# A third pair of score-row buffers, a 136-column memory update and a new order table in an Infini-attention and FNet kernel

## The chip, the cores and the metric

The kernel runs on one NeuronCore of one Trainium2 chip. The metric is the device time of one launch in microseconds (us); the time before is the median of three runs. Engines are named as in the profile: PE (matrix multiply, with PEld for the loads of its stationary operand), DVE (vector), ACT (scalar), POOL (GpSimd) and SP, whose queue issues all the DMAs here.

## What is computed

The input `x` is 2048 rows of 512. Two layers follow each other, each of them a memory attention `A` and a Fourier mixing `B`, both on a layer-normed input and both with a residual:

```python
x = x + _A_ref(_layernorm(x), wq, wk, wv, wo, beta)
x = x + _B_ref(_layernorm(x), dft_seq_re, dft_seq_im, dft_hid_re, dft_hid_im)
...
# A: 32 heads of width 16, 4 segments of 512 rows
for s in range(N):
    qs, ks, vs = q[:, :, s], k[:, :, s], v[:, :, s]
    logits = einsum("bhqd,bhkd->bhqk", qs, ks) * scale + mask     # causal
    a_dot = einsum("bhqk,bhkd->bhqd", softmax(logits), vs)
    pq = phi(qs)                                                   # t+1 or exp(t)
    a_mem = einsum("bhld,bhde->bhle", pq, M) / (einsum("bhld,bhd->bhl", pq, z)[..., None] + 1e-6)
    outs.append(g * a_mem + (1.0 - g) * a_dot)
    pk = phi(ks)
    M = M + einsum("bhld,bhle->bhde", pk, vs)
    z = z + einsum("bhld->bhd", pk)
# B: y = Cr @ (x @ Hr^T) - Ci @ (x @ Hi^T)
```

## The kernel before

**Units of work.** A layer has four segments of 512 rows and four groups of 8 heads, so there are 32 units `i` (segment `q = i // 4`, group `g = i % 4`). All products that need accuracy are made of fp16 pairs: a value is split into a high half and a low half, and three matmuls (`mm3`, line 370) replace one. For a unit the kernel makes q and k (`s_p`, line 784), writes their split halves to DRAM and reads them back in another arrangement, two heads of a pair in partitions 0 to 47 and 64 to 111 (`t_split`, line 681). The tiles that receive them are the row buffers `qst` and `kst`, two of each (`NR = 2`), taken in turn as `i % NR`.

**Scores, maxima, probabilities.** `s_x` (line 895) makes the scores with queries on partitions, and DVE takes the maximum of each row (`t_max`, line 884, 32 instructions for a unit; each writes a `junk` tile of which there are two). The maxima are transposed on PE, split, and sent by DMA into two more rows of `qst`. `s_st` (line 946) then makes the scores once more, transposed and with the maximum subtracted; ACT takes the exponential and POOL the causal mask (`t_sel`). `s_av` (line 969) multiplies the probabilities with the values: the stationary operand is `vt`, 32 columns in fp32 (16 values of a head and 16 ones, whose product is the softmax denominator), and four heads go to four column groups of the array. A buffer pair comes free when `s_st` of its unit is done: in `t_split`, line 703, unit `i` waits on `("ST", i - 2)` before its read-back is issued.

**Memory.** `s_mem` (line 838) reads the memory of a group (`macc`) and updates it: for segments 0 to 2 of each layer, 24 units in all, four matmuls with `phi(k)` as stationary operand stream `vt`, which is laid out per pair of heads as values, ones, values (3 x 16 columns, times 4 pairs: 192 columns in fp32). DVE multiplies the result by the block mask `bd`. In the trace every fp32 matmul stands as two instructions.

**Start.** The layer norms of a segment are in `t_ln` (line 585): statistics on DVE, three small instructions on POOL, then ACT, and a subtraction on POOL or DVE, whichever the planner finds free (`tt`, line 360). For the first segment of each layer (`direct`) the result is transposed on PE. Beside this the weights are loaded into parts of the tile `y`, scaled and split (`s_w`, `s_wo`, `share`). `vt` and `y` are plain SBUF tiles; `y` is free of other use in rows 8 to 11 from the time that the value weights are split until segment 2 writes its rows.

**What sets the order.** Instructions of an engine run in the order in which the program issues them. That order is found at build time: the streams (`s_...`) and tasks (`t_...`) are generators that yield at each step what engine and data they need, and a planner (`Plan`, line 50) with a cost for each instruction picks the step that can start first. The table `LEAN` (line 33) adds a bias in ns for a stream and engine (`t_splitV=-40` puts DVE's step of `t_split` 40 ns behind). Where PE would be idle for long the planner puts in matmuls without use (`t_warm`, line 1216, tile `onesb`). Changing any cost or bias can change the order of the whole program.

Of the kernel before, what the change touches and what calls it, by code (L numbers as in the profile page):

```python
# [19 lines left out]
TT = L // 128  # L20
# [12 lines left out]
LEAN = dict(s_stT=150.0, s_memV=40.0, s_wV=80.0, s_rY=150.0, t_mergeA=40.0, s_xA=150.0, t_abA=40.0, t_mergeY=-150.0, s_mV=40.0, t_cV=-40.0, s_cA=-80.0, s_oY=40.0, t_cY=80.0, t_lnG=80.0, t_splitV=-40.0, t_phiA=150.0, s_kV=-300.0, t_mergeV=150.0, s_cT=80.0, s_avT=80.0, s_wA=-150.0, t_resV=-150.0, t_selG=40.0, s_lnY=-150.0, t_rowsY=300.0, t_ktY=-80.0)  # L33
# [9 lines left out]
PHM, EARLYLN, FEW = 5, 1, 0  # L43
WARM, IDLE, SPARE = 4200, 500.0, 300.0
# [5 lines left out]
class Plan:  # L50
# [31 lines left out]
    def key(self, a):  # L82
        f = self.fine.get(a.tensor.name)
        return (a.tensor.name, a.offset // f) if f else a.tensor.name
# [70 lines left out]
    def op(self, eng, name, args, kw):  # L155
# [19 lines left out]
        elif eng == "A":  # L175
            c = n / 1.2 + (52 if src else 93) + (93 if any(a.free_size() == 1 for a in ins) else 0)
        elif eng == "V":
# [9 lines left out]
        elif eng == "G":  # L187
            c = 127 + n * 0.915 if name == "affine_select" else 96 + n * 2.1
            if name == "tensor_tensor" and kw.get("op") == OP.pow:
                c = 300 + n * 165  # L190
            elif name == "partition_all_reduce":
                c = 370
# [86 lines left out]
def body(ctx: ExitStack, tc: tile.TileContext, x, wq, wk, wv, wo, beta, wd, cs, out):  # L279
# [61 lines left out]
    vt = [const.tile([128, TT, NP, 3, 16], F32, name=f"vt{i}") for i in range(NR)]  # L341
# [5 lines left out]
    bd = const.tile([128, 2, 4, 32], F32, name="bd")  # L347
# [65 lines left out]
    def share(o, src, s):  # L413
        yield need("A", src, s)
        A.activation(o[:, 0], src, AF.Copy, scale=s)
        A.activation(src, src, AF.Copy, scale=s)
        yield need("VG", o, src)
        tt(o[:, 1], src, o[:, 0], OP.subtract)

# [105 lines left out]
    def t_ones():  # L525
# [8 lines left out]
        for i in range(NR):  # L534
            for a in range(2):
                yield need("Y", d8, mode="b")
                Y.dma_start(kst[i][64 * a + 48:64 * a + 50].rearrange("r p n -> r (p n)"), d8, est=(415, 341, 472))
        done.add("KR")

    def s_k():  # L540
# [12 lines left out]
        for j in range(NR):  # L553
            V.memset(vt[j][:, :, :, 1, :], 1.0)
        done.add("VI")
        yield need("V")
        bits(rp, 3, 1.0)
        bits(ra, 64, 1.0 / 64)
        cj = sb("en", F32, (128, 2, 4, 32))
# [25 lines left out]
    def t_ln(src, xi, dst, key, direct=False):  # L585
        st = rg("bst", 2, F32, (128, 6))
        V.bn_stats(st, src)
        mv = rg("mv", 6, F32, (128, 4))
        V.bn_aggr(mv[:, 0:2], st)
        yield need("G", mv)  # L590
        rs = rg("rs", 6, F32, (128, 1))
        G.tensor_scalar(mv[:, 2:3], mv[:, 1:2], 1e-5, 2.0 ** -20, op0=OP.add, op1=OP.mult)
        G.tensor_tensor(rs, mv[:, 2:3], mhalf, op=OP.pow)
        G.tensor_scalar(mv[:, 3:4], mv[:, 0:1], rs, -1.0, op0=OP.mult, op1=OP.mult)
# [6 lines left out]
        else:  # L601
            A.activation(hl[:, 0], xi, AF.Copy)
        yield need("VG", xi, hl)
        tt(hl[:, 1], xi, hl[:, 0], OP.subtract)
        pl.close(xi)
        if direct:
# [7 lines left out]
            if pl.free["A"] <= pl.free["V"]:  # L614
# [36 lines left out]
    def t_merge(e, o, gi, g, n, key):  # L651
# [7 lines left out]
        rc = rg("rc", 4, F32, (128, 2, 16))  # L659
        xa = x[:, 0]  # L660

        def view(off, *dims):
            return bass.AP(xa.tensor, xa.offset + off, [list(xa.ap[0])] + [list(d) for d in dims])

        yield need("V", x)
        d = view(16, (496, 2), (32, 16))
        if not gi:
            V.tensor_scalar(rc, d, 1e-6, None, op0=OP.add)
            d = rc
# [4 lines left out]
        for a in range(2):  # L674
            c = slice(16 * a, 16 * a + 16)
            tt(n.rearrange("p (b r) -> p b r", r=32)[:, :, c], view(528 * a, (32, 16), (1, 16)),
# [4 lines left out]
    def t_split(p, key, f, kphi):  # L681
# [24 lines left out]
        dst = (qst if order else kst)[i % NR]  # L706
# [621 lines left out]
```

## Time and profile before

| | |
|---|---|
| time, median of 3 runs | 1695.57 us (1693.65 to 1700.11) |
| the profiled execution's own time | 1699.92 us |
| its span, first to last instruction | 1698.2 us |
| mean granted TensorE clock in it | 0.989 |
| PE busy | 1662.3 us (98%) |
| DVE, ACT, POOL busy | 1036.8, 872.3, 810.3 us |

The page of the profile gives busy times, the span in 40 slices, the chain of work that ended last and the costliest groups. A row of a group holds, behind the bar, busy time and mean ns of one instruction, and behind the second bar the idle time before. A row of the timeline holds the start, the length of the run, the engine, the instruction with its output and inputs, and its count; brackets give idle time before it and what ended it. A row of the table by stretches gives busy time and count for each engine, the granted clock, the DMA share and GB/s. Nearly all instructions go through one helper and so have one line (L272); they are told apart by tile. In the profile's names a matmul `b<-kst,qst` with 48 rows is one of `s_x`, and `b<-qst,kst` with 50 rows is one of `s_st`; `b<-w,vt` is `s_av`, `b<-vt,w` the memory update.

### The profile page before, as it was taken

The numbers are of one execution on the slowest core, as the hardware profiler recorded it, in microseconds if no ns is written. First come the engines' busy times: TensorE is split into PE (matmuls) and PEld (weight loads), VectorE is DVE, ScalarE is ACT, GpSimd is POOL, SyncE is SP. The second block draws the span as 40 slices with busy tenths as digits, with TensorE's granted clock in tenths as the row PEclk, the third lists the DMA queues.
The fourth block names the chain that finished last, engine by engine and source line by source line (L and its number), as shares of the span: only waits on it lengthen the run. The fifth ranks groups of instructions, "written<-read, shape, count | busy, mean of one in ns | idle before, by whom it ended". The sixth has DMA issues, their size and how long they took to land.

```text
span 1698.2 us, 32247 instructions
## 1 busy us (share of the span) xinstructions
PE 1662.3 (98%) x11145; PEld 734.7 (43%) x11145; DVE 1036.8 (61%) x3262; ACT 872.3 (51%) x1480; POOL 810.3 (48%) x1445
## 2 busy tenths in 40 slices
PE   8889999999999999999999999999999999999999
PEld 4344344444444344444544444443444444444444
DVE  8784865778677786635768558546575765433221
ACT  5487577755656666535376754655455325312000
POOL 4376556575565556634255644635454415322000
PEclk9789999999999999999999999999999999999999
DMA  7546545655357432525746663543435322131423
GB/s 182 147 116 178 128 132 159 172 142 152 94 148 208 126 119 84 189 56 196 193 148 187 182 179 90 132 116 98 140 91 149 105 85 76 57 125 38 143 70 123
DMA packets 208629, 222.92 MB, mean 131 GB/s; under 512 B 104520, under 2 KB 127048, under 8 KB 208464
## 3 DMA queue, kind: packets, MB, share of 16 engines
q1 hardware_dynamic: 208464, 220.85, 45.8%
q8 instruction: 88, 1.44, 0.4%
q14 instruction: 77, 0.63, 0.1%
HBM read 137.40 MB, written 61.87 MB: 117 GB/s over the span
## 4 chain that ended last, share of the span: by engine, by line
PE 77%; DVE 9%; ACT 5%; issue 4%; DMA 3%; POOL 2%; SPq 1%; ACTq 0%; DVEq 0%; POOLq 0%
PE b L272 77%; ACT w L272 4%; DVE junk L272 4%; SPq L272 1%; DVE w L272 1%; POOL w L272 1%; DMA w<-w 1%; DMA w<-x 1%; DVE m L272 1%; DVE mx L272 1%; DVE y L272 1%; DVE bst L272 0%; DVE cam L272 0%; DMA w<-in_cs_dram 0%; DVE pmax L272 0%
## 5 line engine op out<-in xcount | busy, mean ns | idle before, releaser
L272 PEld LDWEIGHTS <-w 128*128 128x128 f16 x5056 | 467.8, 98 | 612.8 <-issue 101.1
L272 PE MATMUL b<-w,w 128*128 128x512 f16 x3072 | 708.5, 380 | 1.7 <-DVE mx L272 0.8
L272 ACT ACTIVATE w<-b,fac 128x512 f32<-128x512 f32 (+1 forms) x728 | 419.2, 655 | 176.3 <-PE b L272 175.8
L272 DVE CUSTOM_DVE_ANT_0 junk<-b,cmask 128x128 bf16<-128x128 f32 (+3 forms) x1024 | 436.3, 483 | 71.6 <-PE b L272 71.1
L272 POOL TENSOR_TENSOR w<-w,w 128x512 f16<-128x512 f32 (+1 forms) x294 | 347.5, 1187 | 247.1 <-ACT w L272 223.6
L272 POOL TENSOR_SCALAR_AFFINE_SELECT w<-w 128x128 f32<-128x128 f32 (+2 forms) x704 | 237.0, 350 | 202.7 <-ACT w L272 194.1
L272 DVE SCALAR_TENSOR_TENSOR y<-b,fyu,y 128x512 f32<-128x512 f32 x200 | 148.9, 745 | 235.6 <-PE b L272 235.2
L272 ACT ACTIVATE w<-w,csc 128x512 f16<-128x512 f32 (+1 forms) x256 | 180.1, 720 | 41.5 <-DVE csc L272 32.8
L272 PE MATMUL b<-g,w 128*128 128x512 f16 x768 | 183.1, 383 | 3.2 <-DMA g<-w 0.8
L272 PE MATMUL b<-wd,w 128*128 128x512 f16 x768 | 176.8, 379 | 0.1
L272 PE MATMUL b<-w,vt 128*32 128x512 f32 (+3 forms) x2048 | 172.4, 449 | 1.9 <-POOL w L272 1.1
L272 ACT ACTIVATE w<-b 128x512 f16<-128x512 f32 x128 | 75.9, 596 | 189.4 <-PE b L272 179.3
L272 DVE SCALAR_TENSOR_TENSOR w<-b,w 128x512 f16<-128x512 f32 x128 | 87.6, 687 | 120.3 <-ACT w L272 118.7
L272 ACT ACTIVATE w<-w 128x512 f16<-128x512 f32 (+1 forms) x137 | 86.5, 632 | 90.1 <-DVE w L272 87.9
L272 PE MATMUL b<-kst,qst 48*128 48x128 f16 (+3 forms) x1024 | 117.5, 304 | 6.3 <-DVE mx L272 3.2
L272 PE MATMUL b<-qst,kst 50*128 50x512 f16 (+3 forms) x1024 | 115.8, 302 | 5.5 <-DVE mx L272 2.2
L272 PE MATMUL b<-w,g 128*128 128x128 f16 x1536 | 96.3, 221 | 0.0
L272 PEld LDWEIGHTS <-g 128*128 128x128 f16 x1536 | 89.6, 99 | 12.7 <-issue 7.8
L272 DVE STREAM_TRANSPOSE m<-b 128x512 f32<-128x512 f32 x112 | 75.6, 698 | 31.1 <-PE b L272 30.7
L272 PEld LDWEIGHTS b<-w,vt 128*32 128x32 f32 x2048 | 54.8, 110 | 87.7 <-issue 48.2
L272 PE MATMUL b<-wo,w 128*128 128x512 f16 x384 | 89.1, 379 | 0.0
L272 PEld LDWEIGHTS <-kst 50*128 50x128 f16 x1024 | 37.3, 94 | 111.7 <-issue 105.2
(105 smaller groups left out, 1019.3 us busy)
## 6 DMA issues: line engine op xcount, KB each, us to landing
w<-in_cs_dram SPq DMA_DIRECT2D x128, 256.0 KB, 3.5
cc<-w SPq DMA_DIRECT2D x128, 256.0 KB, 3.2
w<-cc SPq DMA_DIRECT2D x128, 256.0 KB, 3.1
w<-w SPq DMA_DIRECT2D x96, 256.0 KB, 3.5
d<-w SPq DMA_DIRECT2D x128, 128.0 KB, 2.5
w<-in_x_dram SPq DMA_DIRECT2D x32, 256.0 KB, 3.6
qst<-d SPq DMA_DIRECT2D x64, 128.0 KB, 2.7
kst<-d SPq DMA_DIRECT2D x64, 128.0 KB, 3.3
```

The costliest lines, as they stand in the source:

```text
L272: r = f(*args, **kw)
```

## The change

The title given with the change is: third pair of row buffers for group 2, update by 136 columns, first norms on DVE, steps of one tile apart, new table; two junk tiles for the maxima. The line of the junk tiles is the same in both kernels (two).

- **Row buffers.** A third `kst` and `qst` lie in rows 8 to 11 of `y`, for unit 2 alone (`ring`). Unit 2 waits for the value weights (`("W", 2, g)`) in place of `("ST", 0)`; unit 3 waits on `("ST", 0)` and unit 4 on `("ST", 1)`; from unit 5 on it is two units back as before.
- **Update.** `vt` becomes [tile, 32, 8]: 16 value columns and 16 columns of ones, each by 8 heads, with the heads innermost. The update streams 17 x 8 = 136 columns. `s_av` takes the 32 columns of a head at a step of 8 elements (32 bytes). The value weights are permuted on the host to suit, and ACT writes `vt` in one stretch. DVE's mask step reads the result at a step of 8, once for the values and once, broadcast, for the ones; `bd` becomes bf16.
- **First norms.** For `direct` norms two of the three small instructions go to DVE, and so does the subtraction.
- **Steps apart.** Extra `yield`s (`YL`, `YB`, `YM`, `YC`, `YS`) let the planner put other work between dependent instructions of one tile.
- **Planner.** A new `LEAN`, more cost for an ACT instruction with a bias tile, more latency for small POOL instructions, a preference for DVE in copying the first transposes, and unused matmuls before the causal mask is there.
- **Buffers.** `mx`, `mhl` and `rc` have half as many.

```diff
-LEAN = dict(... t_abA=40.0, ... s_oY=40.0, ... s_cT=80.0, ...)
+LEAN = dict(... t_abA=150.0, ... s_cT=150.0, ... s_ldY=300.0, t_lnA=80.0, t_lnY=-150.0)
...
+            if name == "activation" and isinstance(kw.get("bias"), bass.AP):
+                c += 80
...
+            if n <= 32:
+                lat = 172
...
-    vt = [const.tile([128, TT, NP, 3, 16], F32, name=f"vt{i}") for i in range(NR)]
+    kst.append(y[:, 8:10, :].bitcast(F16).rearrange("p a (b n) -> p (a b) n", n=512))
+    qst.append(y[:, 10:12, :].bitcast(F16).rearrange("p a (b n) -> p (a b) n", n=512))
+    ring = [0, 1, 2] + [(i - 3) % 2 for i in range(3, NGRP)]
+    prior = [None] * 3 + [0, 1] + list(range(3, NGRP - 2))
+    vt = [const.tile([128, TT, 32, HG], F32, name=f"vt{i}") for i in range(NR)]
...
-    bd = const.tile([128, 2, 4, 32], F32, name="bd")
+    bd = const.tile([128, 2, 4, 32], BF16, name="bd")
...
         A.activation(o[:, 0], src, AF.Copy, scale=s)
+        if YC:
+            yield need("A", o)
         A.activation(src, src, AF.Copy, scale=s)
...
+        if direct and STARTV:
+            yield need("V", mv)
+            V.tensor_scalar(mv[:, 2:3], mv[:, 1:2], 1e-5, 2.0 ** -20, op0=OP.add, op1=OP.mult)
+            yield need("G", mv)
+            G.tensor_tensor(rs, mv[:, 2:3], mhalf, op=OP.pow)
+            yield need("V", mv, rs)
+            V.tensor_scalar(mv[:, 3:4], mv[:, 0:1], rs, -1.0, op0=OP.mult, op1=OP.mult)
...
-        yield need("VG", xi, hl)
-        tt(hl[:, 1], xi, hl[:, 0], OP.subtract)
+        if direct:
+            yield need("V", xi, hl)
+            V.tensor_tensor(hl[:, 1], xi, hl[:, 0], op=OP.subtract)
+        else:
+            yield need("VG", xi, hl)
+            tt(hl[:, 1], xi, hl[:, 0], OP.subtract)
...
-        if i >= NR:
-            yield gate(("ST", i - NR))
+        if i == NR:
+            yield gate(*[("W", 2, g) for g in range(NG)])
+        elif i > NR:
+            yield gate(("ST", prior[i]))
...
-        A.activation(vt[i % NR].rearrange("p t j e d -> p (t j) e d")[:, :, 0:3:2, :],
-                     p.rearrange("p t (j e d) -> p (t j) e d", j=NP, e=2), AF.Copy, scale=2.0 ** -24)
+        A.activation(vt[i % NR].rearrange("p t d h -> p t (d h)")[:, :, :128], p, AF.Copy, scale=2.0 ** -24)
...
-                mp = ps("pj", F32, (128, NP, 48))
+                mp = ps("pj", F32, (128, 17, HG))
...
-                    T.matmul(mp, phk[:, 128 * t:128 * t + 128], v[:, t], start=(t == 0), stop=(t == TT - 1))
+                    T.matmul(mp, phk[:, 128 * t:128 * t + 128], v[:, t, :17], start=(t == 0), stop=(t == TT - 1))
...
-                for a in range(2):
-                    V.tensor_tensor(mu[:, a], mp[:, :, 16 * a:16 * a + 32], bd[:, a], op=OP.mult)
+                for e, d in ((0, HG), (16, 0)):
+                    V.tensor_tensor(view(mu, e, (128, 2), (32, NP), (1, 16)),
+                                    view(mp, HG * e, (NP, 2), (1, NP), (d, 16)),
+                                    view(bd, e, (128, 2), (32, NP), (1, 16)), op=OP.mult)
...
-            mx = rg("mx", 2, F32, (128, 2, NP, TT))
+            mx = rg("mx", 1, F32, (128, 2, NP, TT))
...
-                                 v[:, t, p].rearrange("k e d -> k (e d)")[:, 16 * a:16 * a + 32], tiles[p][1],
+                                 v[:, t, :, NP * a + p], tiles[p][1],
...
-        if "CM" not in done or at - pl.free["T"] < IDLE or pl.lately(at) >= WARM:
+        if at - pl.free["T"] < IDLE or pl.lately(at) >= WARM:
```

More of the change, by code (lines that the diff above doesn't have):

```diff
@@ L418, in share, with view @@
         tt(o[:, 1], src, o[:, 0], OP.subtract)
+    def view(t, off, *dims):
+        return bass.AP(t.tensor, t.offset + off, [list(t.ap[0])] + [list(d) for d in dims])
     def flat(t):
@@ L658, in t_merge @@
         pl.close(e, o)
[L659 to L663, printed above, removed]
+        rc = rg("rc", 2, F32, (128, 2, 16))
         yield need("V", x)
[L666 removed]
+        d = view(x, 16, (512, 2), (32, 16))
         if not gi:
             V.tensor_scalar(rc, d, 1e-6, None, op0=OP.add)
+            if YM:
+                yield need("V", rc)
             d = rc
@@ L701, in t_split @@
             spawn(t_kt(hl, kphi))
-        if i >= NR:
-            yield gate(("ST", i - NR))
+        if i == NR:
+            yield gate(*[("W", 2, g) for g in range(NG)])
+        elif i > NR:
+            yield gate(("ST", prior[i]))
         yield need("Y", d)
         order = key[0] == "dq"
-        dst = (qst if order else kst)[i % NR]
+        dst = (qst if order else kst)[ring[i]]
         for a in range(2):
```

55 lines of the change are left out of this document (38 added, 17 removed).

## Prediction

> **What bounds the kernel now.** First the page: which engine is never free, and where its clock falls. Then the table by stretches, which says whether PE's idle time is spread or in one place.
>
> ```profile
> span 1698.2 us, 32247 instructions
> PE 1662.3 (98%) x11145; PEld 734.7 (43%) x11145; DVE 1036.8 (61%) x3262; ACT 872.3 (51%) x1480; POOL 810.3 (48%) x1445
> PEclk9789999999999999999999999999999999999999
> ```
>
> ```profile
> 0.00:20.00 20.00, 14.34 (x77) 6.53 (x78) 16.96 (x53) 9.84 (x12) 10.07 (x25) 1.00 0.82 211
> 20.00:45.00 25.00, 24.22 (x197) 12.96 (x195) 23.38 (x93) 13.92 (x24) 8.10 (x7) 1.00 0.67 157
> 45.00:140.00 95.00, 83.78 (x587) 33.78 (x586) 69.08 (x270) 68.47 (x120) 58.90 (x112) 0.82 0.46 125
> 200.00:1600.00 1400.00, 1387.91 (x9435) 612.28 (x9434) 864.91 (x2673) 742.78 (x1262) 696.33 (x1241) 1.00 0.45 129
> 900.00:1000.00 100.00, 97.84 (x725) 44.43 (x726) 65.21 (x224) 63.18 (x108) 56.42 (x102) 1.00 0.64 180
> ```
>
> From 200 to 1600 us PE idles 12.1 of 1400 us at full clock: what PE does there is paid for one to one, and what the other engines do there is free until one of them becomes late. The start is different. From 45 to 140 us PE idles 11.2 of 95 us and the granted clock is 0.82, so another 0.18 x 95 = 17 us of cycles are gone, and its 587 instructions are 6.2 a us against 9435 / 1400 = 6.7 later. This part is held by something else. So the change has two places to act: PE's own work anywhere, and the chain of the start.
>
> **The update.** These rows hold what the narrower update is worth: 24 units x 4 matmuls x 2 instructions.
>
> ```profile
> L272 PE MATMUL b<-vt,w 128*128 128x192 f32 x192 | 38.6, 338 | 1.4 <-ACT vt L272 1.2 <-POOL w L272 0.2
> L272 PEld LDWEIGHTS b<-w,vt 128*32 128x32 f32 x2048 | 54.8, 110 | 87.7 <-issue 48.2 <-POOL w L272 23.4 <-DVE mx L272 3.0
> L272 PEld LDWEIGHTS b<-vt,w 128*128 128x128 f32 x192 | 30.9, 190 | 10.7 <-issue 2.7 <-DVE mx L272 2.3 <-ACT vt L272 1.6
> ```
>
> ```profile
> 75.16 1.07 PE L272 MATMUL b<-w,vt 128*32 128x512 f32 x8
> 79.55 1.57 PE L272 MATMUL b<-vt,w 128*128 128x192 f32 x8
> 81.05 0.85 PE L272 MATMUL b<-w,vt 128*32 128x384 f32 x8
> 82.16 0.92 PE L272 MATMUL b<-vt,w 128*128 128x192 f32 x4
> ```
>
> The mean of 338 ns holds the way through the array, which overlaps. The pace is in the runs: (1.57 - 0.92) / 4 = 162.5 ns each, 0.85 ns a column. 136 columns then take 115 ns, 47 ns less, and 192 x 47 ns = 9.1 us, all in PE's time. One thing could stop it short: the load of the next stationary operand. A 128-column fp32 load takes 190 ns and a 32-column one 110, so 80 / 96 = 0.83 ns a column and 107 ns for 128 columns: still under 115. I take -9.1 us. ACT's write of `vt` and DVE's mask step keep their element counts and are off PE's path; ends 0 and, if each of the 48 mask instructions were late on an idle PE, a few us in the start, so 0.
>
> **Weights at a step of 32 bytes.** `s_av` pays for the same layout: each head's 32 fp32 weights now lie 8 elements apart. The trace has only packed loads: 54.8 us / 2048 = 27 ns each where they run one behind the other. A burst of `s_av` is four heads in two rounds. The second round's loads lie under the first round's stream: 512 columns and 384 columns differ by 0.22 us over two rounds, so 128 columns take 0.11 us a round. Only the first loads of a burst are open, and there are 32 units x 4 tiles x 2 halves = 256 bursts. A load of n times the length costs 256 x 27 x (n - 1) ns: 0 for n = 1, 6.9 us for n = 2, 28 us for n = 5. A gain is excluded, since packed loads are the best case here. I take 0, the row that the trace has, and keep 6.9 us for the range.
>
> [...]
>
> **The third buffer pair.** What did unit 2 wait for? PE first: the end of unit 1's maxima (the transpose of `mx`), the last scores of `s_st` of unit 0, and the units 2 and 3 of `s_x`. Then SP and DVE.
>
> ```profile
> 69.74 0.39 PE L272 MATMUL b<-identf,mx 128*32 128x128 f32 x1 [1.56 <-DVE mx L272]
> 83.01 0.40 PE L272 MATMUL b<-qst,kst 50*128 50x128 f16 x8
> 90.67 0.42 PE L272 MATMUL b<-kst,qst 48*128 48x128 f16 x8
> 112.56 0.27 PE L272 MATMUL b<-identf,mx 128*32 128x128 f32 x1
> 113.44 0.61 PE L272 MATMUL b<-kst,qst 48*128 48x128 f16 x12
> 131.24 0.27 PE L272 MATMUL b<-identf,mx 128*32 128x128 f32 x1 [0.94 <-ACT w L272]
> 138.71 2.10 PE L272 MATMUL b<-g,w 128*128 128x512 f16 x9
> ```
>
> ```profile
> 72.97 2.63 SPq L272 DMA_DIRECT2D d<-w  x4
> 75.70 1.36 SPq L272 DMA_TRANSPOSE w<-w  x1
> 77.11 0.57 SPq L272 DMA_DIRECT2D w<-in_x_dram  x1
> 79.76 3.05 SPq L272 DMA_DIRECT2D d<-w  x4
> 83.43 1.74 SPq L272 DMA_DIRECT2D qst<-d  x4
> 85.21 1.81 SPq L272 DMA_DIRECT2D kst<-d  x4
> ...
> 104.04 1.71 SPq L272 DMA_DIRECT2D qst<-d  x4
> 110.14 0.46 SPq L272 DMA_DIRECT2D w<-in_x_dram  x1
> ```
>
> ```profile
> 70.67 0.67 DVE L272 SCALAR_TENSOR_TENSOR w<-b,w 128x512 f16<-128x512 f32 x1
> 71.98 0.69 DVE L272 SCALAR_TENSOR_TENSOR w<-b,w 128x512 f16<-128x512 f32 x1
> 79.04 0.69 DVE L272 SCALAR_TENSOR_TENSOR w<-b,w 128x512 f16<-128x512 f32 x1 [6.37 <-ACT w L272]
> ```
>
> ```profile
> 59.01 1.16 POOL L272 TENSOR_TENSOR w<-y,w 128x512 f16<-128x512 f32 x1 [0.21 <-ACT y L272]
> ```
>
> ```profile
> d<-w SPq DMA_DIRECT2D x128, 128.0 KB, 2.5
> kst<-d SPq DMA_DIRECT2D x64, 128.0 KB, 3.3
> ```
>
> The read-back of unit 2 is issued at 83.43, at the end of `s_st` of unit 0 (83.01 + 0.40). So the wait is real. But behind it stands another: DVE makes the low halves of unit 2 only at 70.67 and 71.98, after all maxima of unit 1, and the write to DRAM leaves SP at 72.97 to 75.60 and lands 2.5 us later, at 78.1. `t_splitV` stays at -40 in the new table, so I leave that order. With the gate gone the read-back can be issued at 78.1, behind the transpose and the x load that SP holds until 77.7; it takes 1.74 + 1.81 us, and the last part lands 3.3 us after its issue, at about 85. Unit 2's scores start there and not at 90.67: 5.4 us sooner. They then take what they took, 112.56 - 90.67 = 21.9 us, and so end at 107; unit 3's read-back, which waits for `s_st` of unit 0 and no more for that of unit 1 (SP stands before 104.04 for it), is then long there, so the 5.4 us pass on to unit 3. SP also carries the x load of 110.14 behind that wait; the norm made from it opens segment 1's projection at 138.71. So at least 5.4 us, and at most 90.67 - 69.74 = 21 us if unit 2 could follow unit 1 directly; DVE's 6.37 us of idle time before 79.04 shows that there is room for part of it. I take 8 us, near the lower end since that is worked out row by row. The moved DMAs push the `d<-w` at 79.76 by about 2 us, which unit 3 has to spare. What is moved ahead is paid back in full, since PE is full from 200 us on. The gate on the value weights costs 0: the last subtraction that reads a weight staged in `y` before the scores of unit 2 ends at 59.01 + 1.16 = 60.2, 18 us ahead of need. So do the two more DMAs that write rows of ones into the third `kst`, about 0.6 us each on SP by the row at 77.11.
>
> **First norms.** The first real matmul on `g` starts at 16.88.
>
> ```profile
> 10.41 3.38 POOL L272 TENSOR_TENSOR w<-w,w 128x512 f16<-128x512 f32 x3
> 14.15 1.16 POOL L272 TENSOR_TENSOR w<-w,w 128x512 f16<-128x512 f32 x1 [0.36 <-DVE w L272]
> 16.88 1.46 PE L272 MATMUL b<-g,w 128*128 128x512 f16 x6 [0.68 <-ACT g L272]
> ```
>
> POOL's four subtractions, 4.5 us, go to DVE, where two of this form take 1062 ns each in the group list:
>
> ```profile
> L272 DVE TENSOR_TENSOR w<-w,w 128x512 f16<-128x512 f32 x2 | 2.1, 1062 | 5.8 <-ACT w L272 5.8
> ```
>
> DVE is itself busy 16.96 of the first 20 us, so a chain on POOL becomes one on DVE of 4.2 us. Ends -2 us (POOL's chain gone) and +2 us (DVE's in its place); I take 0. At the start of layer 2 PE has other work.
>
> **Table, planner, spacing, fewer buffers.** They add no PE work. From 200 to 1600 us the order can win back at most the 12.1 us of idle time; were every stretch as poor as 900 to 1000 (2.2 us idle in 100) it would lose 14 x 2.2 - 12.1 = 18 us. The new biases touch seven entries of some thirty, and gaps between dependent instructions on DVE, ACT and POOL are free where those engines are idle 38 to 50% of the time. I take 0, with 6 us to each side. One `mx` in place of two makes the first maximum of a unit wait for the transpose before it; unit 2 starts long after it in these rows, so 0.
>
> **Sum.** -9.1 - 8 + 0 = -17 us: the profiled execution's own 1699.92 would become 1683. It stands 4.3 us above the median of the runs; the same step from 1695.57 gives **1679 us**, 1.0% less. A measurement of this kernel can tell about 0.5%, 8.5 us, from no change.
>
> **The rivals.**
> - *The start does not move.* Unit 2 follows DVE's late split, and what the buffers free is given back on SP or DVE. For it: 70.67 and 71.98 above. Against: the issue at 83.43 right at the end of `s_st` 0. Then -9 us alone: 1686.5, on the edge of what can be told; an order that loses a few us puts it within 0.5%.
> - *The start moves by all of it.* Unit 2's split comes ahead of unit 1's maxima and its scores follow at 70: -9 - 21 = -30 us, 1665. For it: DVE idle before 79.04, and the x load that SP frees. Against: the bias of the split is the old one.
> - *A stepped load takes twice its time.* If each weight at the new step costs a second read, 256 x 27 ns = 6.9 us are open: 1679 + 7 = 1686. For it: nothing in the trace, since no load has a step. [...]
> - *A stepped load takes five times its time (the slower side).* 256 x 107 ns = 27 us, and the 0.11 us rounds of the 128-column tiles no longer cover the second round's 0.13 us, 64 x 27 ns = 2 us more: 1679 + 29 = 1708. It decides from n = 4.7, where 1704 is passed. [...]
>
> **How the numbers follow.** The forecast's own case (gain in the start of 5 to 12 us, loads unchanged) gets 0.55; the large gain 0.06; the start that does not move 0.17, of which 0.04 is faster by over 0.5%; the doubled load 0.10, half of it faster; the fivefold load 0.12. Faster 0.55 + 0.06 + 0.04 + 0.05 = 0.70, same 0.13 + 0.05 = 0.18, slower 0.12. The range goes down to 1661 (the large gain with a few us from the order) and up to 1700 (no gain in the start, doubled loads, 6 us lost to the order); the fivefold load is left out.
>
> **What would show it.** Right: update instructions with 136 columns and a pace of 115 ns in their runs; unit 2's first 48-row scores near 85 us and its `mx` transpose near 107; segment 1's first projection before 131; a clock above 0.82 in 45 to 140; PE still idle about 12 us from 200 to 1600. Wrong: `s_av` bursts of 8 longer than 1.07 and 0.85 us, or their loads longer than 110 ns; PE waits in the middle; a first projection later than 17 us; unit 2 again behind 90 us.

## The result, and the profile after

The changed kernel takes 1712.36 us (median of 4 runs, 1710.25 to 1718.03) against 1696.17 us beside it on the same chip: ratio 1.0099, 95% interval 1.0084 to 1.0114. It is 16 us slower; 1679 us, 1.0% faster, was forecast, and 1700 was the top of the range. The profiled execution took 1718.03 us, 5.7 us above the median; the times that traces show below are those of profiled executions. Times and ratios below leave out one execution of the second experiment, which ran at a granted clock of 0.652 and took 2393.93 us. The changed kernel's page, first the span, then PE's line and PE's granted clock in 40 slices:

```profile
span 1716.3 us, 32342 instructions
PE 1670.6 (97%) x11173; PEld 745.4 (43%) x11173; DVE 1041.3 (61%) x3294; ACT 862.0 (50%) x1478; POOL 791.3 (46%) x1415
PEclk9987999999999999999999999999999999999999
```

The table by stretches (window, its length, busy time of PE, weight loads, DVE, ACT, POOL with their instructions, granted clock, DMA share, GB/s):

```profile
20.00:45.00 25.00, 20.84 (x126) 10.59 (x127) 14.51 (x46) 10.64 (x18) 6.63 (x8) 0.86 0.20 53
45.00:140.00 95.00, 81.70 (x606) 36.07 (x604) 74.62 (x305) 55.82 (x98) 47.30 (x89) 0.87 0.52 135
200.00:1600.00 1400.00, 1385.87 (x9419) 617.30 (x9419) 872.28 (x2707) 741.48 (x1271) 690.84 (x1235) 1.00 0.47 129
900.00:1000.00 100.00, 96.78 (x763) 43.59 (x756) 65.35 (x213) 68.60 (x121) 63.01 (x113) 1.00 0.69 191
```

From 200 to 1600 us PE idles 14.1 us where it idled 12.1: the long middle is as it was. The stretch 20 to 45 us is not: PE has 126 instructions in it where it had 197, and DMA 0.20 of its share where it had 0.67. The groups by form, where the edits on PE show (out, in, array, shape, count, then busy us, mean ns, idle time before):

```profile
L279 PEld LDWEIGHTS b<-w,vt 128*32 128x32 f32 x2048 | 68.0, 145 | 80.4 <-issue 46.5 <-POOL w L279 19.9 <-DVE mx L279 2.8
L279 PE MATMUL b<-vt,w 128*128 128x136 f32 x192 | 30.8, 302 | 1.9 <-POOL w L279 0.8 <-ACT vt L279 0.8 <-ACT w L279 0.2
```

The update has its 136 columns, and the loads of `s_av` take 145 ns where they took 110. PE's timeline at the places that the prediction named (start, length, what, count, idle time before and what ended it):

```profile
30.88 6.97 PE L279 MATMUL b<-g,w 128*128 128x512 f16 x24 [2.27 <-DVE bits L279]
...
100.39 0.39 PE L279 MATMUL b<-y 48*128 48x128 f16 x8
...
112.98 1.19 PE L279 MATMUL b<-vt,w 128*128 128x136 f32 x8
...
121.24 0.73 PE L279 MATMUL b<-vt,w 128*128 128x136 f32 x4 [0.80 <-ACT vt L279]
122.09 0.28 PE L279 MATMUL b<-identf,mx 128*32 128x128 f32 x1
122.21 0.63 PE L279 MATMUL b<-vt,w 128*128 128x136 f32 x4
127.80 0.58 PE L279 MATMUL b<-y 50*128 50x512 f16 x1 [4.96 <-DMA y<-mhl]
...
146.66 4.14 PE L279 MATMUL b<-g,w 128*128 128x512 f16 x18
```

The first projection starts at 30.88 and not at 16.88. (Its row names `bits`, the first step of the group mask, which the change also holds back: a gate in `s_k` that the list of the change does not name. What the projection reads is the copy just ahead of it on DVE, at 30.05 below.) Unit 2's scores start at 100.39, not near 85, and its `mx` transpose is at 122.09. The update's pace is (1.19 - 0.73) / 4 = 115 ns. Then PE waits 4.96 us for the row of maxima `mhl`, and segment 1's first projection is at 146.66 where it was at 138.71. DVE's and SP's timelines say why at both places:

```profile
9.93 0.17 DVE L279 BATCH_NORM_AGGREGATE mv<-bst 128x2 f32<-128x6 f32 x1
...
11.13 0.15 DVE L279 TENSOR_SCALAR mv<-mv 128x1 f32<-128x1 f32 x1
...
16.37 2.46 DVE L279 TENSOR_REDUCE vm<-y 128x1 f32<-128x512 f32 x4
18.86 0.16 DVE L279 TENSOR_REDUCE amax<-vm 128x1 f32<-128x4 f32 x1
18.94 1.68 DVE L279 TENSOR_TENSOR w<-w,w 128x512 f16<-128x512 f32 x1
20.54 0.20 DVE L279 TENSOR_SCALAR mv<-mv,rs 128x1 f32<-128x1 f32 x1
...
25.83 1.39 DVE L279 TENSOR_TENSOR w<-w,w 128x512 f16<-128x512 f32 x1
...
30.05 0.68 DVE L279 COPY g<-b 128x1024 f16<-128x1024 f16 x1
30.65 0.14 DVE L279 TENSOR_SCALAR bits<-pi 128x1 int32<-128x1 int32 x1
```

```profile
110.28 0.97 SPq L279 DMA_DIRECT2D w<-in_x_dram  x2
123.99 1.24 SPq L279 DMA_TRANSPOSE g<-w  x1
125.32 2.51 SPq L279 DMA_DIRECT2D y<-mhl  x4
```

The norm of tile 4 has its statistics at 9.93 and its first small step on DVE at 11.13, but the second comes only at 20.54 and its subtraction at 25.83: these steps stand in DVE's queue behind the splits of group 0's weights and the reductions over weights that nobody needs yet. SP stands from 111.25 to 123.99 before a norm's transpose, and the four writes of unit 2's maxima, for which PE waits, stand behind it.

**Where the time goes.** The order of the work differs, so one instruction's shift says little. The table below counts PE's work instead: each matmul of a trace, without the unused ones, with the median time to the next matmul that its form has in the kernel before after 250 us; it shows by how many us a kernel is behind the time at which the kernel before had done as much (its own profiled execution, 4.3 us above its median). PE's work comes in bursts, so a number up to 160 us can be off by 2 or 3 us, a later one by less than 1. The names of the other columns are the experiments below.

```
at us    after  start   gap    all mended  old order  new table  old order
                queues  filled and packed  to 48 us   alone      throughout
   30     12.5    5.1    12.5      4.1        3.2        1.0         3.0
   60     15.1   15.1    15.1     11.4        9.0        1.3         2.5
  120      7.0    6.6     6.6      6.8        3.2        6.3        -0.5
  160     12.4   11.0     7.3      7.3        4.4        1.5         0.5
  220     20.4   19.3    11.4     13.4       16.4        9.9         2.2
  700     16.6   16.2    10.5     10.2       18.8       18.1         5.5
 1000     13.6   10.3     6.7      5.0       15.9       21.6         4.7
 1680     18.3   10.5     8.3      1.9       29.1       26.7         3.4
```

In the changed kernel 15 us are lost by 60 us. Half of them come back by 120, 13 more are lost up to 220, and from there it is carried to the end.

### The profile page after: what moved, and what is told of

It reads as the page before. It is cut to its first block, busy times and chain, and to the rows that moved or that the text cites. A ratio compares the mean times of both kernels' runs of the same rounds, so it can differ in the third digit from the quotient of the medians.

```text
span 1716.3 us, 32342 instructions
## 1 busy us (share of the span) xinstructions
PE 1670.6 (97%) x11173; PEld 745.4 (43%) x11173; DVE 1041.3 (61%) x3294; ACT 862.0 (50%) x1478; POOL 791.3 (46%) x1415
## 4 chain that ended last, share of the span: by engine, by line
PE 80%; DVE 6%; DMA 4%; ACT 4%; issue 3%; SPq 1%; POOL 1%; ACTq 0%; DVEq 0%; POOLq 0%
PE b L279 80%; ACT w L279 3%; DVE junk L279 2%; DMA w<-w 2%; SPq L279 1%; POOL w L279 1%; DVE w L279 1%; DVE mx L279 1%; DVE y L279 0%; DMA w<-in_cs_dram 0%; DVE pmax L279 0%; DMA w<-cc 0%; DVE cam L279 0%; DMA g<-w 0%; DVE m L279 0%
## 5 line engine op out<-in xcount | busy, mean ns | idle before, releaser
L279 POOL TENSOR_TENSOR w<-w,w 128x512 f16<-128x512 f32 (+1 forms) x283 | 334.1, 1188 | 193.7 <-ACT w L279 171.7
L279 ACT ACTIVATE w<-w,csc 128x512 f16<-128x512 f32 (+1 forms) x256 | 175.5, 723 | 25.2 <-DVE csc L279 18.7
L279 PE MATMUL b<-qst,kst 50*128 50x512 f16 (+1 forms) x992 | 112.2, 300 | 6.8 <-ACT w L279 3.5
L279 PE MATMUL b<-kst,qst 48*128 48x128 f16 (+1 forms) x992 | 113.2, 304 | 4.7 <-ACT w L279 1.3
L279 PEld LDWEIGHTS b<-w,vt 128*32 128x32 f32 x2048 | 68.0, 145 | 80.4 <-issue 46.5
L279 PEld LDWEIGHTS <-g 128*128 128x128 f16 x1536 | 89.0, 99 | 15.6 <-issue 6.3
L279 DVE DVE_READ_ACCUMULATOR2_ANT mx<- 128x1 f32 x1024 | 85.1, 83 | 0.1
```

Of the source, the lines that this page charges most:

```text
L279: r = f(*args, **kw)
```

## The experiments

Theory A before them: the first norms on DVE delay the first projection, and that is the loss. Its rivals: the stepped loads (B), the order in the start, and later (O) that each edit makes the planner write another order, and that the order is what costs.

**First norms back on POOL** (all else as changed):

```diff
-STARTV, YL, YB, YM, YC, YS = 1, 1, 1, 1, 1, 1
+STARTV, YL, YB, YM, YC, YS = 0, 1, 1, 1, 1, 1
-        if direct:
+        if direct and STARTV:
```

> The changed kernel with the first norms as before: the three small instructions on POOL, the subtraction wherever the planner finds room; all else of the change stays. Theory A (the norm steps on DVE stand behind the weights' reductions, so that the first projection starts at 30.9 us and not at 16.9, and the 14 us are never won back): first projection on g at 15 to 19 us, time 14 to 18 us under the changed kernel, 1694 to 1698 us. Theory B (the loss is the stepped weight loads or the new order after 45 us): the first projection moves but the time stays within 5 us of the changed kernel's 1712.

Measured: 1725.46 us, ratio 1.0184 (1.0167 to 1.0202). The first projection is back at 17.72, and the kernel is slower still. Its list of PE's waits has a line of the kind that showed above, longer:

```profile
PE b L279 <- DMA y<-mhl: 8.5, 1, 8.5
```

Theory A falls as stated: the step that it blamed is gone and the loss is not.

**First norms first on DVE**: one more bias in the table.

```diff
-... t_lnA=80.0, t_lnY=-150.0)
+... t_lnA=80.0, t_lnY=-150.0, t_lnV=300.0)
```

> The changed kernel with one more entry in the table, t_lnV=300, so that DVE takes the steps of a norm ahead of the weights' reductions; the norms stay on DVE. Theory A (it is the place in the order, not the engine): first projection at 15 to 18 us, time 1692 to 1698 us. Rival A2 (DVE has too much to do in the first 30 us, whatever the order): first projection after 22 us, time over 1703 us. Theory B: time stays near 1712 us.

Measured: 1711.89 us, 1.0101 (1.0085 to 1.0116): theory A's 1692 to 1698 missed again. The first projection is at 18.39, yet unit 0's first scores start at 40.84 where they started at 34.39: now the split of unit 0's k stands on DVE behind weight reductions and the group mask. Any such edit makes the planner write all of the order anew, so from here on the order is held: either the planner is given the old costs of changed instructions, so that it writes the old order, or the steps are run from a written-out list (the helper's line is then L574 or L575, in one kernel L558).

**The value tile stepped, update left at 192 columns, in the old order**, and **the update at 136 in the same order**:

```diff
-    vt = [const.tile([128, TT, NP, 3, 16], F32, name=f"vt{i}") for i in range(NR)]
+    vt = [const.tile([128, TT, 32, HG], F32, name=f"vt{i}") for i in range(NR)]
-                    T.matmul(mp, phk[...], v[:, t], ...)
+                    T.matmul(mp, phk[...], v[:, t, :24], ...)    # second kernel: :17
-                                 v[:, t, p].rearrange(...)[:, 16 * a:16 * a + 32], tiles[p][1],
+                                 v[:, t, :, NP * a + p], tiles[p][1],
```

> The kernel before in its own order, instruction by instruction, with the value tile laid out as in the changed kernel (weights of a head 8 elements apart) but with the update still streaming 192 columns (values, and 8 of the 16 rows of ones). Theory C (a stepped load takes 35 ns longer, as 110 and 145 ns in the two profiles say, and it lies open once in each of 256 bursts): loads of 145 ns, time 1696 + 9 = 1705 us, PE runs of 8 instructions at 512 columns 1.10 in place of 1.07 us. Rival D (the loads are covered by the stream): loads of 145 ns and time within 2 us of 1696.

> As the run with 192 stepped columns, in the same order as the kernel before, with the update at 136 columns. The update alone is worth 192 x 47 ns = 9.1 us in every theory, so 9 us under that run: 1696 us by theory C, where the edit of the value tile is worth nothing, and 1687 us by rival D, where it is a gain of 0.5%.

Both kernels, and the packed one after them, also have the smaller `mx`, `mhl` and `rc`, the bf16 `bd` and twice as many ones in `vt`; every engine runs the old order.

Measured: 1698.59 us, 1.0024 (1.0013 to 1.0035), and 1696.35 us, 1.0006 (0.9994 to 1.0018). The load in the first, by form:

```profile
L272 PEld LDWEIGHTS b<-w,vt 128*32 128x32 f32 x2048 | 68.9, 144 | 79.1 <-issue 45.6 <-POOL w L272 21.3 <-DVE mx L272 2.7
```

A load at a step of 32 bytes takes 144 ns on average, and with this tile the kernel is 0.24%, 4 us, longer: between theory C's 9 and rival D's 2. The narrower update takes the time from its matmuls to the next from 34.8 to 25.8 us, 9.0 as forecast, but the kernel gains 0.18%, 3 us. In the two traces the other 6 us come back as longer steps of the 48- and 50-row scores (4.0 us) and of the value projection (1.5): PE's busy time falls only from 1661.7 to 1657.7. So theory C's 1696 for the second kernel came out by luck, as 4 less 3 and not as 9 less 9.

**The same with packed weights**, `vt` as `[128, TT, HG, 32]`, the load reading `v[:, t, 2 * p + a]` and the update streaming `v[:, t, :, :17]`:

> The kernel before in its own order, the value tile as 16 heads of 32 words (each head's 32 weights lie side by side), and the update streams the 17 words per head that it needs, 8 x 17 = 136 columns. Against the run with the stepped tile and the same order and update (1696.35): if the step of 32 bytes costs what the table by form showed there (about 2.8 us of the 1696), this gives about 1693.5, with the load of s_av's weights back at 110 ns and the update still at 25 to 26 us of PE time. If the moving operand pays for its own breaks every 17 words, the update's run of eight is longer than 1.19 us and the time stays at 1696 or above. If the 9 us that the update no longer needs are worth their full size when the loads are packed, it gives 1687.

Measured: 1694.83 us, 0.9993 (0.9983 to 1.0004); loads at 110 ns and 54.7 us again, update as before. It is the fastest version of the study, and a measurement can't tell it from the kernel before.

**The third pair alone, in the old order**, with its read-back and unit 2's scores moved ahead:

```diff
 SP:  d<-w (unit 2), transpose, x load
+     y<-d x10 (ones rows, read-back of unit 2)
      d<-w (unit 3)
-     qst<-d x4, kst<-d x4 (read-back of unit 2)
 PE, DVE: scores and maxima of unit 2 each 30 steps earlier
```

> The kernel before in its own order with one part alone: group 2's row buffers are a third pair, its read-back stands on SP ahead of unit 3's write, and the scores and maxima of unit 2 stand 30 steps (about 4 us) earlier in the queues of PE and DVE; two ones rows more are written. Value tile, update, norms as before. The prediction's term for the start (unit 2 waits for its buffers, 5.4 us of them worked out row by row, all of it carried to the end) gives 1688 to 1691. Rival (PE is full between 76 and 115 us, where it idles less than 4 us, so scores that come earlier only push other work of PE back): 1694 to 1698, with unit 2's first scores near 86 and the end unmoved. Slower than 1699 if what is pushed back (projection of values, update) is itself waited for.

Measured: 1700.01 us, 1.0024 (1.0012 to 1.0036).

```profile
87.37 0.40 PE L558 MATMUL b<-y 48*128 48x128 f16 x8
...
115.39 0.42 PE L558 MATMUL b<-identf,mx 128*32 128x128 f32 x1
```

The scores start 3.3 us sooner than at 90.67, the maxima are done 2.8 us later than at 112.56, and the kernel is 4 us slower, the third of the cases written down. SP and this unit had waited for the buffers, but PE had other work. With the scores moved ahead PE idles 6.0 us between 90 and 116 where it idled 3.0, in short waits for DVE's maxima, ACT and POOL. This is one place for the unit; others were not tried.

**All parts of the change, in the old order.** Each engine's instructions stand where the old order has them; the first norms' steps come to DVE at POOL's places, and the group mask's bits come as early as they did. Two things are missing by this: the new order's further unused matmuls (83 in all, as before, and not 111), and any use of the third pair, whose read-back keeps its old place on SP (86.04; unit 2's scores start at 93.82).

> The changed kernel with every part of the change (value tile stepped, update by 136 columns, third pair, first norms on DVE, single junk tiles), but each engine's instructions stand in the order of the kernel before; only the first norms' steps come to DVE instead of POOL, at the places where POOL had them, and two ones rows are added. Theory O (the parts cost little, the order that the planner wrote anew for them costs the rest): 1695 to 1699, near the run with the stepped tile and 136 columns in the old order (1696.35). Rival P (the parts themselves cost it): 1708 to 1713. Rival Q (the first norms are too much for DVE): first projection later than 20 us and 1700 to 1705.

Measured: 1699.33 us, 1.0022 (1.0011 to 1.0033). The first projection:

```profile
20.06 1.46 PE L574 MATMUL b<-g,w 128*128 128x512 f16 x6 [0.68 <-ACT g L574]
```

That is 3.2 us later than in the kernel before. With the stepped tile at 136 columns alone, norms still on POOL, it is earlier:

```profile
17.62 1.46 PE L272 MATMUL b<-g,w 128*128 128x512 f16 x6 [0.68 <-ACT g L272]
```

It is at 17.63 with the packed tile and at 18.54 with 192 columns. So about 1 us comes with the value tile, whose memset of ones ahead of the first statistics takes 1.02 us where it took 0.55, and about 2 with the norms on DVE. The run with all parts decides between orders and parts: with them, old order 0.22% above the kernel before, new order 0.99%; the intervals lie apart, and rival P's 1708 to 1713 is out. Between theory O and rival Q it does not: 1699.33 lies between O's 1699 and Q's 1700, and 20.06 just past Q's 20. **Packed**, the same kernel:

> The kernel of the run before this one in this call with the value tile packed as 16 heads of 32 words. The step of 32 bytes cost 1.5 us (old order) and 3.4 us (new order) so far, so 1693 to 1697; the best version if no part of the change costs anything in this order.

Measured: 1698.20 us, 1.0012 (1.0002 to 1.0022), 1 us above what was expected.

**The start's queues rearranged**, the rest of the new order held, and the same **with packed weights**:

```diff
 DVE: ... split of group 0's weights
-     reductions over group 1, the value weights, group 2
+     norms of tiles 3 and 4
      ...
-     norms of tiles 3 and 4
+     reductions over group 1, the value weights, group 2, between the projections of units 0 and 1
```

> The changed kernel, its whole order kept instruction by instruction, but for the first 35 us: there the steps of the norms of tiles 3 and 4 stand ahead of the reductions over the second to fourth group's weights, and the projections of group 0 follow them, with the weight reductions between. No work is added or taken. Theory O (the loss is made by the order of the queues in the start and is then carried): first projection at 17 to 18 instead of 30.88, the first maxima's transpose 10 to 14 us earlier than in the changed kernel, and the time falls by 10 to 14 us, to 1698 to 1702. Rival P (the parts themselves cost it: stepped loads, one step apart on DVE, POOL and ACT, unused matmuls): the first projection moves, the end does not, 1709 to 1713. Rival Q (the first norms on DVE are too much work for DVE): first projection not before 24, 1705 or more.

> The kernel of the run before this one in this call (changed kernel with its start's queues reordered), and the value tile packed as 16 heads of 32 words, in the same order. If the step of 32 bytes costs 2.8 us here as in the other order, this is 2 to 4 us below that run; if a load that is late is hidden in this order, there is no difference (within 1 us).

Measured: 1710.04 us, 1.0073 (1.0054 to 1.0093), and 1706.61 us, 1.0058 (1.0041 to 1.0075). The first projection is at 20.23, but the first maxima's transpose is at 60.11, against 62.84 in the changed kernel and 48.26 in the kernel before: most of the lead is gone by then. By the numbers written down this is rival P's case, and theory O's 1698 to 1702 missed. PE and SP say why the lead is lost:

```profile
20.23 2.69 PE L575 MATMUL b<-g,w 128*128 128x512 f16 x6
...
35.90 0.38 PE L575 MATMUL b<-amax,ones 128*128 128x2 f32 x2 [4.10 <-DVE amax L575]
```

```profile
27.74 11.29 SPq L575 DMA_DIRECT2D d<-w  x6
```

The write of unit 1 that this order puts ahead of unit 0's read-back waits on SP for its split. So this is no clean trial of the start: one wait was traded for others, and 28 unused matmuls are gone from it (83 for 111). Its 0.26% is not clear of the noise either. Packing gives 0.13%, 0.10% and here 0.15%, some 2 us in each of three orders; each alone is within the noise or at its edge, and the three agree.

**Old order up to 48 us, and up to 95 us, then the new one:**

> All parts of the change; the order of the kernel before up to the last scores of unit 0 (about 48 us), from there on the remaining instructions in the changed kernel's own order. If the loss is made before 48 us and then carried: transpose of the first maxima at 48 to 50 instead of 62.9, and the end 12 to 15 us below the changed kernel, 1697 to 1701. If each stretch of the new order loses on its own, only a part comes back: 1702 to 1709. If PE catches up whatever the start does, 1710 to 1713.

> As the run before this one in this call, with the order of the kernel before up to about 95 us (500 steps instead of 230). Against that run it tells what the new order does between 48 and 95 us, where the third pair lets unit 2 start: if it gains 5 us there (the prediction's term), this is 5 us above the other; if it only permutes a full PE, both agree within 2 us; if the new order loses there too, this is lower, 1695 to 1698.

Measured: 1732.24 us, 1.0210 (1.0192 to 1.0228), and 1748.39 us, 1.0306 (1.0289 to 1.0323). Every case that was written down missed. In the first the start is mended (3.2 us behind at 30 us, 9.0 at 60, 3.2 at 120), yet 13 us are lost by 220 as in the changed kernel, and 13 more by the end. These two orders could not be cut and joined at either place. A likely reason, not shown: what comes after the joint was ordered for buffers and engines that come free at other times.

**The norms of segment 1 earlier**, with the projection that they feed and without:

```diff
 SP, DVE, POOL, ACT: x loads and norms of tiles 5 to 8 each 85 steps earlier
 PE: (first kernel alone) first projection of segment 1 100 steps earlier
```

> The changed kernel in its own order, with one stretch rearranged: the x loads and norms of segment 1 (tiles 5 to 8) stand 85 steps (about 15 us) earlier in the queues of SP, DVE, POOL and ACT, and the first projection of segment 1 stands 100 steps earlier on PE. No work is added or taken. Theory S (between 120 and 220 us the new order loses 13 us because it brings the four norms of segment 1 together and late, so that PE stands with nothing queued but what waits for the row of maxima behind a norm's transpose on SP, and its clock falls): PE's wait at 123 to 128 us gone, clock in 120 to 140 above 0.8, progress behind the kernel before at 220 us down from 20 to about 8 to 12 us, and the time 1700 to 1705. Rival (the stretch only shows a lateness that was made before it): no change, 1710 to 1714.

> As the run before this one in this call, but PE's order is left alone: only the loads and norms of segment 1 stand earlier. Theory S, if SP's blocked queue is what counts: the writes of unit 2's maxima no longer stand behind the norm's transpose, PE's wait of 5 us shrinks to 2 to 3 us and the time falls by 2 to 5 us, 1707 to 1710. If what counts is that PE has no projection queued to fill the gap, the wait and the time stay within 2 us of the changed kernel, 1710 to 1714.

Measured: 1727.53 us, 1.0188 (1.0174 to 1.0202), and 1717.88 us, 1.0138 (1.0124 to 1.0152). Both are slower than the changed kernel. SP's and PE's timelines of the second:

```profile
126.41 2.62 SPq L575 DMA_TRANSPOSE g<-w  x2
129.12 2.50 SPq L575 DMA_DIRECT2D y<-mhl  x4
```

```profile
131.66 0.58 PE L575 MATMUL b<-y 50*128 50x512 f16 x1 [6.53 <-DMA y<-mhl]
```

Two transposes now stand ahead of the maxima, and the wait is 6.53 us (6.98 in the first). Both moves went the wrong way, and all cases written down missed. In this order a longer wait here goes with a slower kernel (4.96, 6.53 and 6.98 us with 1712, 1718 and 1728); since the moves changed other waits too, that is a hint and no proof.

**The gap filled**, at that place alone:

```diff
 SP:  x loads
+     y<-mhl x4
      DMA_TRANSPOSE g
-     y<-mhl x4
 DVE: second half of mhl ahead of steps of two norms
 PE:  transpose of mx
+     first 16 scores of unit 3 (s_x)
      first 8 transposed scores of unit 2 (s_st)
```

> The changed kernel in its own order, rearranged at one place only, where PE waits 4.96 us from 122.8 us: the writes of unit 2's maxima stand ahead of the norm's transpose on SP and their second half ahead of two norms' steps on DVE, and the first three score steps of unit 3 stand ahead of unit 2's weighted scores on PE. No work is added or taken. Theory S' (a gap of 5 us on PE costs its own length and then the clock's half speed for 20.5 us from 126.4): wait at 122 to 129 us 0 to 2 us, clock in 120 to 140 above 0.75 instead of 0.66, and 1704 to 1709. Rival (what is filled here is waited for elsewhere, since SP, DVE and POOL are as late as before): the wait moves, and the time stays 1710 to 1714.

Measured: 1708.02 us, 1.0071 (1.0059 to 1.0083).

```profile
121.59 0.40 PE L575 MATMUL b<-kst,qst 48*128 48x128 f16 x8
122.69 0.61 PE L575 MATMUL b<-kst,qst 48*128 48x256 f16 x4 [0.70 <-DVE macc L575]
125.12 0.59 PE L575 MATMUL b<-onesb 128*128 128x512 bf16 x1 [1.83 <-DVE mx L575]
```

The wait of 4.96 us is now two, 0.70 and 1.83, and 0.28% of the time, 5 us, comes back. The table by stretches of the kernel before, of the changed one and of this one:

```profile
120.00:140.00 20.00, 17.44 (x122) 5.24 (x122) 11.56 (x37) 18.39 (x34) 14.42 (x31) 0.83 0.27 70
```

```profile
120.00:140.00 20.00, 12.37 (x58) 4.27 (x55) 14.84 (x68) 13.33 (x24) 13.86 (x26) 0.66 0.07 14
140.00:160.00 20.00, 19.74 (x131) 6.50 (x130) 7.93 (x22) 17.57 (x33) 13.10 (x26) 0.83 0.83 211
```

```profile
120.00:140.00 20.00, 16.42 (x74) 4.62 (x74) 17.49 (x78) 15.95 (x28) 17.46 (x33) 0.57 0.33 68
140.00:160.00 20.00, 19.68 (x175) 9.30 (x177) 7.52 (x14) 19.26 (x35) 14.12 (x29) 1.00 0.79 212
```

PE is busy for 4 us more of the 20 from 120 to 140. The clock is lower in them, 0.57 where above 0.75 was expected and 0.66 in the changed kernel, and full after them, 1.00 for 0.83 from 140 to 160. So the time came out as expected, and the sign of the clock did not. **Start, packing and gap together:**

> The rearranged start (the run with the start's queues reordered), the packed value tile and the filled gap of the first run of this call, all in the changed kernel's order. If the three add up, 1706.6 (start and packed) less what the gap gives, 1700 to 1704; if the gap gives nothing, 1705 to 1708.

Measured: 1701.61 us, 1.0031 (1.0019 to 1.0044). Within the intervals the three add up: 0.26% + 0.15% + 0.28% of the 0.99% would leave 0.30%.

**The new table alone on the kernel before, and one bias of the old table moved by 5 ns:**

```diff
-LEAN = dict(s_stT=150.0, ..., t_abA=40.0, ..., s_oY=40.0, ..., s_cT=80.0, ...)
+LEAN = dict(s_stT=150.0, ..., t_abA=150.0, ..., s_cT=150.0, ..., s_ldY=300.0, t_lnA=80.0, t_lnY=-150.0)
```

```diff
-... s_cT=80.0 ...
+... s_cT=85.0 ...
```

> The kernel before with the new table of biases and nothing else of the change: same instructions, another order. If the order is the whole loss and the table made it, this is as slow as the changed kernel or slower, 1708 to 1730. If the new order comes of all edits together (norm steps, gates, costs), the table alone stays within 5 us of 1696.

> The kernel before with one bias moved by 5 ns (the one of the transposes that sum up the sequence factors, 80 to 85): same instructions, the order differs from about the middle of PE's queue on. It measures what another order of the same work is worth when nothing speaks for or against it. If orders are that sensitive, it lies 3 to 15 us off 1696, to either side; if only bad orders in the start matter, within 2 us.

Measured: 1726.17 us, 1.0174 (1.0159 to 1.0189), and 1697.97 us, 1.0014 (1.0004 to 1.0025). The table alone, with no other edit, costs 30 us. Its loss lies elsewhere: 9.9 us behind at 220, 18.1 at 700, 26.7 at the end. The list of PE's waits names the maxima on DVE (total, number, longest), first in the kernel before, then here:

```profile
PE b L272 <- DVE mx L272: 10.6, 19, 1.6
```

```profile
PE b L272 <- DVE mx L272: 22.6, 44, 2.4
```

That is 12 us more, less than half of the loss; the rest has no place yet. The nudge moves the order only from the middle of PE's queue on, and is worth 2 us, between the two cases written down.

## Why the prediction was wrong

**The step that failed** is the one that gave table, planner and spacing "0, with 6 us to each side". Its working looked only at 200 to 1600 us, where PE's 12.1 us of idle time bound a gain, and called seven biases (they are six) of some thirty few. Shown: the new order with the same parts costs 13 us (0.99% against 0.22%), and the table alone, under the old parts, 30. Which of the edits wrote the bad order is not isolated. Nor do they "add no PE work": 111 unused matmuls stand where 83 stood. In the changed kernel it costs most where the prediction had not looked for it, before 220 us. The rows for a better bound were there: 45 to 140 us had 11.2 us of idle PE and 17 us of lost clock, so waits take a share of this stretch, and an order can add to them as well as take them away.

**First norms, "0", ends -2 and +2.** The work was costed nearly rightly: at POOL's places the norms on DVE put the first projection about 2 us later. Their place in the queue was not costed. A step moved to DVE also waits for whatever the planner puts between its steps there (tile 4's three stand at 11.13, 20.54 and 25.83 us), and the projection came 14 us later. The text read that DVE is busy for 16.96 of the first 20 us, but counted only the chain's own 4.2 us, not the reductions over weights that it would stand behind.

**Third pair, -8.** The rows were read rightly up to the read-back: without the gate it can be issued at 78. The step "the 5.4 us pass on" failed, in the one place that was tried: unit 2's scores did not take the same 21.9 us as before but 28.0, between PE's other work, so the pair alone moved unit 2's maxima 2.8 us later. In the new order unit 2's scores follow unit 1's maxima (transpose at 84.82) by 15.6 us where they followed by 20.9, the 5.4 us almost to the digit, and PE makes up 8 us between 60 and 120; that these two belong together is argued, not shown. There the pair's read-back is issued only from 91.97 on, since SP stands from 70.99 to 85.35 before a write to DRAM; the prediction had costed SP only for the pair's own DMAs.

**Update, -9.1.** The size is right, 9.0 us of PE. "All in PE's time" is not: 3 us of it reach the end in the old order. PE's busy share is 98% with and without these 9.0 us, and 5 of them went into longer steps of other matmuls, so a busy PE is not yet paid "one to one".

**Stepped loads, 0.** The rival "twice its time" was nearer: 145 ns for 110, 4 us by the run with the tile's layout changed at 192 columns, and some 2 us by packing. The factors two and five were the author's assumptions, and no run shows either: in the changed kernel the loads are busy for 68.0 us where they were for 54.8, 1.24 times as long. Packed loads are the shorter ones of the two layouts that ran, 110 ns for 144 in the old order. The fivefold load, which carried the slower side, did not happen: that the kernel came out near its 1708 is luck.

**What stays open.** 0.31% is left when start, packing and gap are mended, and 0.12% is what the packed parts cost in the old order; the 3 us between have no place. How much of the start's 15 us reaches the end was not isolated, since the one kernel that mended the start alone traded it for a wait on SP. The old biases under the new parts were not tried, nor the new order without the third pair or without its further unused matmuls.

## What to carry to other kernels

Where a planner writes the order, every edit is two edits: the instruction, and a new order of the whole program. Hold the order and change the part, then hold the parts and change the order, before either is judged; and bound the order's term by the stretch with idle PE and lost clock, not by the full one. When a step moves to another engine, write down which instructions will stand ahead of it in that queue, SP's included, and who waits for those behind it.

## What the runs showed of the hardware

In the changed kernel PE ran nothing from 122.84 to 127.80, a gap of 4.96 us, and the granted clock was 0.50 for 20.5 us from 126.4 on. Three rows of its table by stretches, out of that time:

```profile
134.00:137.40 3.40, 3.24 (x12) 0.62 (x10) 3.40 (x19) 3.06 (x5) 0.58 (x2) 0.50 0.00 0
137.40:140.80 3.40, 3.31 (x10) 0.72 (x9) 3.40 (x15) 3.40 (x8) 3.19 (x4) 0.50 0.25 48
140.80:144.20 3.40, 3.40 (x16) 0.72 (x19) 2.96 (x10) 3.37 (x7) 2.90 (x7) 0.50 1.05 189
```

PE is busy for 9.95 of these 10.2 us, and the clock stays at 0.50. Of the whole 20.5 us PE is busy for 17.29, with 48- and 50-row scores and 32-column matmuls for most of them; from 146.9 to 160 the clock is 1.00. What brings it back, no run isolates.

A DVE subtraction of 128x512 took 1.68 us at 18.94 in the changed kernel, while POOL ran one of its own, and 0.68 at 12.65 in the run with all parts in the old order, while POOL ran nothing. Whether POOL is the reason, no run isolates.
